# Decode attention plus MLP on one core: the attention's output weights loaded behind the last V tiles, and the MLP's last weight in three pieces

## The chip, the cores and the metric

The kernel runs on one core of one Trainium2 chip. The metric is the device time of the whole program in microseconds, taken over several executions; the profile is one further execution, and its span is about 2 us shorter than the timed figure. PE is the tensor engine, DVE the vector engine, ACT the scalar engine, and SP the sync engine, which issues the loads. The granted clock is the share of PE's full clock that its throttle let through. Times inside a profile are microseconds from the start of its span.

## The reference, cut to what matters

One decode step for 8 sequences: LayerNorm, attention with 32 query heads over 8 KV heads and the last 2048 cache positions, the output projection `wo`, then a block of LayerNorms and an MLP with weights `w3` and `w4`. Each sequence has one token, so the token-shift branch of the MLP block is zero and `w1`, `w2` drop out.

```python
def _A_ref(x, k_cache, v_cache, wq, wo):          # x: 8 x 1 x 512
    W = 2048                                      # last 2048 of 8192 positions
    q = (x @ wq) ...                              # 32 heads of 128
    k, v = k_cache[:, :, Sk-W:], v_cache[:, :, Sk-W:]
    p = softmax(q @ k.T * 128**-0.5)
    return (p @ v).reshape(8, 1, 4096) @ wo       # wo: 4096 x 512
def _B_ref(x, ...):
    x1 = x                                        # the shifted branch is zero
    return x1 + gelu(layernorm(x1) @ w3) @ w4     # w3: 512 x 1792, w4: 1792 x 512
h = x + _A_ref(layernorm(x), ...)
out = h + _B_ref(layernorm(h), ...)
```

K and V are 2 x 33.6 MB of the 79.2 MB that the kernel reads; wo is 4.2 MB, w3 and w4 1.8 MB each.

## The kernel before

All loads are issued from SyncE (SP) in one list. They go round through ten slots of 2 MiB; a load waits until the slot's former tile has been used. K and V come as 16 tiles each, four KV heads of one sequence per tile.

```python
WO_CUT = [0, 16, 24, 28, 32]      # heads of each wo piece
WO_HALF = H // 2
W4_CUT = [0, 8, 14]               # row groups (128 rows) of each w4 piece
V_CUT = [0, C // 2, C]            # the last V tile comes in two halves
order = [("k", 0), ("k", 1)]
for b in range(NB - 1):
    order += [("k", 2*b+2), ("v", 2*b), ("k", 2*b+3), ("v", 2*b+1)]
order += [("wo", 0), ("v", NTILE-2), ("v", NTILE-1), ("wo", 1), ("w3", 0), ("w4", 0)]

for n, (kind, t) in enumerate(order):             # on SP
    free_slot(n)                                  # waits for the user of order[n - 10]
    ...
    elif kind == "wo":                            # rows of 512 bf16, 1 KB each
        ... e.dma_start(dst[...], A_wo[h0*128:h1*128, :].rearrange("(h p) n -> p h n", p=128))
    elif kind == "w3":                            # rows of 3.5 KB
        e.dma_start(w3_sb, B_w3.rearrange("(k p) f -> p k f", k=KC)).then_inc(sem_w3, 16)
    else:                                         # rows of 2 KB
        for i in range(len(W4_CUT) - 1):
            c0, c1 = W4_CUT[i] // 2, W4_CUT[i+1] // 2
            e.dma_start(w4_dst[:, c0:c1, :], w4_rows[:, c0:c1, :]).then_inc(sem_w4[i], 16)
```

The end of the tensor engine's (PE) program, after the last softmax; the line numbers are those of the profile:

```python
# L530  P.V of V tile 14, then 15: 64 matmuls each of 16 columns
# L603  wo: 32 heads x 4 matmuls of 8 columns
for h in range(H):
    if h in WO_CUT:
        e.wait_ge(sem_wo[WO_CUT.index(h)], 16)
    for k in range(KC):
        e.matmul(hT_ps[:, k*B:(k+1)*B], wo_at(h)[:, k*128:(k+1)*128], oT_all[:, h, :], ...)
# L621  statistics of both LayerNorms; DVE and ACT make uT
# L663  w3: 14 x 4 matmuls of 8 columns
e.wait_ge(sem_w3, 16)
for fc in range(FC):
    for kc in range(KC):
        e.matmul(misc[:, H3...], w3_sb[:, kc, ...], uT[:, kc*B:(kc+1)*B], ...)
# ACT: gelu
# L684  the residual; L693  w4: 14 row groups x 2 matmuls of 256 columns
for fc in range(FC):
    if fc in W4_CUT:
        e.wait_ge(sem_w4[W4_CUT.index(fc)], 16)
    for j in range(NQ):
        e.matmul(fin_ps[32*j:32*j+B, :], gT[:, fc*B:(fc+1)*B], w4_sb[:, fc, j*DQ:(j+1)*DQ],
                 ..., tile_position=(0, 32*j))
# DVE and ACT copy the result out, SP stores it
```

## Time and profile before

| | before |
|---|---|
| timed, median (range) | 198.81 us (198.02 to 198.83), 3 runs |
| span of the profile | 196.6 us |
| bytes read | 79.18 MB, 403 GB/s over the span |
| busy: PE, DVE, ACT | 81%, 42%, 46% |

From the page of the kernel before, the span in 40 slices of 4.9 us: the granted tensor clock in tenths, the busy share of the 16 DMA engines in tenths, and what they moved.

```profile
PEclk9999999999996999999999699969999979755557
DMA  6999999999999999999999999999999999999990
GB/s 215 427 410 430 427 430 427 430 430 430 430 422 427 430 425 430 427 430 430 427 427 433 430 430 427 428 423 423 427 430 433 430 388 382 425 405 338 398 358 21
```

The DMA row shows 9 from the second slice to the last but one: the kernel is bound by its load queue for almost the whole span. The rate falls from 430 to between 338 and 425 GB/s near the end, where rows are 1 to 3.5 KB instead of 16 KB, though the engines stay busy. The Trainium skill (DMA: Bandwidth & Descriptors, "Why small descriptors are slow (HBM only)") gives a fixed overhead per packet as a cause; this trace agrees in direction (432 GB/s at 150 to 158 us with 16 KB rows, 352 at 179 to 184.5 with rows of 1 and 3.5 KB) but does not separate the causes. In slices 36 to 39 the clock row shows 5: half clock.

The end of the chain of waits of the kernel before (start, length, what):

```profile
174.82 9.25 DMA slots<-in_A_wo_dram
...
184.12 0.40 PE S_ps L603 x9
184.52 1.93 issue
186.46 0.34 PE S_ps L603 x7
...
191.76 2.64 PE b L693 x28
...
194.42 0.41 DVE xln_b L703
```

"issue" is time in which PE waited for nothing that the profile shows. The timeline of PE at the end of the kernel before (start, length, engine, line, operation, count, and in brackets the idle time ahead of it and what ended that):

```profile
174.16 1.88 PE L530 MATMUL misc<-pT_sb,slots 128*128 128x16 bf16 x64
176.23 1.02 PE L530 MATMUL misc<-pT_sb,slots 128*128 128x16 bf16 x32 [0.18 <-DMA slots<-in_A_v_cache_dram]
178.66 0.97 PE L530 MATMUL misc<-pT_sb,slots 128*128 128x16 bf16 x30 [1.41 <-DMA slots<-in_A_v_cache_dram]
179.86 0.23 PE L530 MATMUL misc<-pT_sb,slots 128*128 128x16 bf16 x2 [0.23 <-issue]
...
184.12 0.40 PE L603 MATMUL S_ps<-oT_all,slots 128*128 128x8 bf16 x9 [0.23 <-DMA slots<-in_A_wo_dram]
186.46 0.33 PE L603 MATMUL S_ps<-oT_all,slots 128*128 128x8 bf16 x7 [1.93 <-issue]
...
189.59 1.64 PE L663 MATMUL misc<-uT,slots 128*128 128x8 bf16 x56 [1.61 <-DVE uT L640]
...
191.58 2.79 PE L693 MATMUL b<-slots,gT 128*8 128x256 bf16 x28
```

V tile 15 is waited for twice (0.18 and 1.41 us), wo's last piece lands at 184.1, 1.93 us go to "issue" before wo's last seven matmuls, and the w4 matmuls (L693) run 2.79 us without a wait. SP's own timeline of the kernel before, around wo part 0:

```profile
125.03 0.39 SPq L266 DMA_DIRECT2D slots<-in_A_wo_dram  x1
127.27 36.10 SPq L260 DMA_DIRECT2D slots<-in_A_v_cache_dram  x1
```

The load of V tile 14 is issued at 127.27, but that instruction takes 36.10 us. The Trainium skill (Perfetto Trace Analysis, "DMA Instruction — HWDGE") says that the time recorded for such an instruction is the wait for the descriptor generator plus the generation, and not the data's movement. That fits here, though the profile does not show what is waited for: the load issued next after wo part 0 (2048 rows of 1 KB) is the one that takes so long, V tile 14.

### The profile page before, as it was taken

What the parts mean: (1) busy time and instruction counts of PE and PEld (TensorE: products, weight loads), DVE (VectorE), ACT (ScalarE), POOL (GpSimd) and SP (SyncE); (2) the same over time, 40 slices, a digit from 0 to 9 for tenths busy, and PEclk for the clock granted to TensorE, in tenths of its full rate; (3) what the DMA queues carried; (4) which work ended last, traced back from release to release, by engine and by line L of the source; (5) the groups of instructions that cost most, each with busy time, mean ns of one, the idle gap of its engine ahead of it and who ended that gap; (6) DMA issues with size and microseconds to landing.
All of it is one profiled execution on the core that took longest, in us unless ns stands there. A gap on an engine that the chain in (4) does not pass through costs nothing.

```text
span 196.6 us, 6327 instructions
## 1 busy us (share of the span) xinstructions
PE 159.2 (81%) x2808; PEld 118.4 (60%) x2808; DVE 82.4 (42%) x184; ACT 90.6 (46%) x109; POOL 4.7 (2%) x15
## 2 busy tenths in 40 slices
PE   2027999789999998988897889899979879395555
PEld 0027865566768675755675667677756656185553
DVE  7501445543463457335623473356336514330040
ACT  3300565945392648434753384457535635240040
POOL 8000000000000000000000000000000000000000
PEclk9999999999996999999999699969999979755557
DMA  6999999999999999999999999999999999999990
GB/s 215 427 410 430 427 430 427 430 430 430 430 422 427 430 425 430 427 430 430 427 427 433 430 430 427 428 423 423 427 430 433 430 388 382 425 405 338 398 358 21
DMA packets 10569, 79.57 MB, mean 405 GB/s; under 512 B 672, under 2 KB 4784, under 8 KB 6192
## 3 DMA queue, kind: packets, MB, share of 16 engines
q1 hardware_dynamic: 10544, 79.19, 96.5%
q8 instruction: 22, 0.36, 0.7%
q14 instruction: 3, 0.02, 0.0%
HBM read 79.18 MB, written 0.01 MB: 403 GB/s over the span
## 4 chain that ended last, share of the span: by engine, by line
DMA 56%; PE 28%; SPq 6%; issue 4%; DVE 3%; ACT 3%; ACTq 0%; DVEq 0%
DMA slots<-in_A_k_cache_dram 51%; PE kT_ps L406 16%; PE S_ps L438 6%; SPq L266 5%; DMA slots<-in_A_wo_dram 5%; PE misc L530 3%; ACT P_sb L472 1%; PE b L693 1%; ACT kT_sb L417 1%; PE misc L663 1%; DVE pT_sb L504 1%; PE S_ps L603 0%; PE S_ps L621 0%; DVE mtile L450 0%; SPq L258 0%
## 5 line engine op out<-in xcount | busy, mean ns | idle before, releaser
L417 ACT ACTIVATE kT_sb<-kT_ps 128x1024 bf16<-128x1024 bf16 x64 | 65.5, 1023 | 75.6 <-PE kT_ps L406 75.6
L406 PEld LDWEIGHTS kT_ps<-ident_b,slots 128*128 128x128 bf16 x1024 | 63.7, 104 | 30.0 <-issue 21.5
L406 PE MATMUL kT_ps<-ident_b,slots 128*128 128x128 bf16 x1024 | 73.2, 231 | 7.9 <-DMA slots<-in_A_k_cache_dram 7.9
L423 DVE COPY kT_sb<-kT_ps 128x1024 bf16<-128x1024 bf16 x64 | 43.4, 687 | 61.4 <-PE kT_ps L406 61.4
L438 PE MATMUL S_ps<-kT_sb,qstrip 128*32 128x512 bf16 x256 | 39.0, 614 | 0.0
L530 PEld LDWEIGHTS misc<-pT_sb,slots 128*128 128x128 bf16 x1024 | 27.3, 97 | 7.7 <-issue 5.9
L530 PE MATMUL misc<-pT_sb,slots 128*128 128x16 bf16 x1024 | 28.6, 170 | 3.7 <-DVE pT_sb L504 1.9
L472 ACT ACTIVATE P_sb<-S_ps,mtile 128x1024 bf16<-128x1024 f32 x16 | 17.8, 1113 | 4.8 <-DVE mtile L461 4.4
L406 PE MATMUL kT_ps<-ident_b,P_sb 128*128 128x128 bf16 x128 | 10.6, 231 | 6.6 <-ACT P_sb L472 5.5
L406 PEld LDWEIGHTS kT_ps<-ident_b,P_sb 128*128 128x128 bf16 x128 | 7.8, 103 | 12.0 <-issue 4.4
L504 DVE TENSOR_TENSOR pT_sb<-kT_ps,maskT 128x1024 bf16<-128x1024 bf16 x16 | 10.4, 684 | 0.1
L438 PEld LDWEIGHTS S_ps<-kT_sb,qstrip 128*32 128x32 bf16 x256 | 6.0, 94 | 6.5 <-issue 1.2
L537 DVE TENSOR_TENSOR oT_all<-misc,rL 128x32 bf16<-128x32 f32 x8 | 2.4, 300 | 16.0 <-PE misc L530 16.0
L585 ACT ACTIVATE std<-var,eps_t 128x8 f32<-128x8 f32 x1 | 0.3, 301 | 14.3 <-DVE var L636 14.3
L450 DVE TENSOR_REDUCE mtile<-S_ps 128x1 f32<-128x512 f32 x8 | 5.5, 692 | 3.1 <-PE S_ps L438 3.1
L361 PE MATMUL S_ps<-xlnT,slots 128*128 128x8 bf16 x128 | 3.6, 168 | 3.6 <-DMA slots<-in_A_wq_dram 3.6
L361 PEld LDWEIGHTS S_ps<-xlnT,slots 128*128 128x128 bf16 x128 | 3.5, 104 | 3.6 <-issue 3.6
L603 PE MATMUL S_ps<-oT_all,slots 128*128 128x8 bf16 x128 | 3.9, 168 | 2.2 <-issue 1.9
L341 PE MATMUL b<-ident_b,xln_b 8*128 8x8 bf16 x4 | 0.3, 175 | 6.4 <-DVE xln_b L318 6.4
L603 PEld LDWEIGHTS S_ps<-oT_all,slots 128*128 128x128 bf16 x128 | 3.6, 104 | 2.3 <-issue 2.0
L481 DVE TENSOR_TENSOR lsum<-lcol 128x1 f32<-128x1 f32 x8 | 1.3, 158 | 8.0 <-ACT P_sb L472 8.0
L341 PEld LDWEIGHTS b<-ident_b,xln_b 8*128 8x128 bf16 x4 | 0.2, 116 | 7.3 <-DVE xln_b L318 7.3
(75 smaller groups left out, 59.8 us busy)
## 6 DMA issues: line engine op xcount, KB each, us to landing
slots<-in_A_k_cache_dram SPq DMA_DIRECT2D x16, 2048.0 KB, 41.5
slots<-in_A_v_cache_dram SPq DMA_DIRECT2D x15, 2048.0 KB, 43.3
slots<-in_A_wq_dram SPq DMA_DIRECT2D x1, 4096.0 KB, 12.2
slots<-in_A_wo_dram SPq DMA_DIRECT2D x1, 2048.0 KB, 43.8
slots<-in_A_v_cache_dram SPq DMA_DIRECT2D x2, 1024.0 KB, 13.6
slots<-in_B_w_dram SPq DMA_DIRECT2D x1, 1792.0 KB, 11.6
slots<-in_A_wo_dram SPq DMA_DIRECT2D x1, 1024.0 KB, 16.5
slots<-in_A_wo_dram SPq DMA_DIRECT2D x2, 512.0 KB, 13.0
```

The source lines that it names most:

```text
L266: e.dma_start(dst[:, f0:f0 + (h1 - h0) * D].rearrange("p (h n) -> p h n", n=D), A_wo[h0 * 128:h1 * 128, :].rearrange("(h p) n -> p h n", p ...
L361: ins = e.matmul(S_ps[:, 0, h * B:(h + 1) * B], wq_v[:, kc, h * DH:(h + 1) * DH], xlnT[:, kc * B:(kc + 1) * B], start=(kc == 0), stop=(kc ...
L406: ins = e.matmul(kT_ps[n % 2][:, c * 128:(c + 1) * 128], src[:, c * 128:(c + 1) * 128], ident_b[:, :], is_transpose=True)
L417: e.activation(kT_sb[:, i % NKT, 0:W // 2], kT_ps[step_of[("k", i)] % 2][:, 0:W // 2], ACT.Copy).then_inc(sem_Elo, 1)
L423: e.tensor_copy(kT_sb[:, i % NKT, W // 2:W], kT_ps[step_of[("k", i)] % 2][:, W // 2:W]).then_inc(sem_Ehi, 1)
L438: ins = e.matmul(S_ps[32 * gl:32 * (gl + 1), b % 2, :], qstrip[:, b, GL * gq + gl, o:o + 32], kv[:, gl, :, :], start=(gq == 0 and qi == 0) ...
L450: ins = e.tensor_reduce(mtile[:, 2, 0:1], S_ps[:, j, :], AX.X, ALU.max)
L472: e.activation(P_sb[:, half * W // 2:(half + 1) * W // 2].rearrange("r (k g) -> r k g", g=GL), s_rep, ACT.Exp, bias=mtile[:, j, 0:1], scal ...
L504: e.tensor_tensor(pT_sb[:, half * hc:(half + 1) * hc, :], kT_ps[n % 2][:, half * W // 2:(half + 1) * W // 2].rearrange("p (c x) -> p c x", ...
L530: ins = e.matmul(ot, slots[:, slot, c * DH:(c + 1) * DH], pt[:, cc, :, o:o + R], start=(n == 0), stop=(n == C - 1), skip_group_check=True)
L537: e.tensor_tensor(oT_all[:, :, b].rearrange("p (q g r) -> p g q r", g=GL, r=R), misc[:, OT].rearrange("p (g q r) -> p g q r", g=GL, r=R), ...
L603: ins = e.matmul(hT_ps[:, k * B:(k + 1) * B], wo_at(h)[:, k * 128:(k + 1) * 128], oT_all[:, h, :], start=False, stop=(h == H - 1), skip_gr ...
```

## The change: intent and diff

wo part 0 (2 MiB) is not needed until attention is over, but it was loaded ahead of the last two V tiles. The change puts it behind them, so that the last P·V no longer waits. And w4 gets a small last piece, so that less work remains when the last bytes land.

```diff
-        sem_w4 = [S(f"sem_w4_{i}") for i in range(2)]
+        sem_w4 = [S(f"sem_w4_{i}") for i in range(3)]
...
-        W4_CUT = [0, 8, 14]
+        W4_CUT = [0, 8, 12, 14]
...
-        order += [("wo", 0), ("v", NTILE - 2), ("v", NTILE - 1), ("wo", 1), ("w3", 0), ("w4", 0)]
+        order += [("v", NTILE - 2), ("v", NTILE - 1), ("wo", 0), ("wo", 1), ("w3", 0), ("w4", 0)]
```

The instructions of PE, DVE and ACT keep their order; only SP's list changes, and PE gets one more wait, before w4's row group 12.

## The prediction

> **What bounds the kernel now.** The load queue, then a latency chain. By slices, the 16 DMA engines are about 99% busy until just before the end; 79.2 MB at 405 GB/s is 195 us of a 196.6 us span. The last weight bytes (w4) move until about 192.6 us (packet records), so this change, which keeps every byte, has 192.6 us as its floor, plus a short tail.
>
> The end of the chain of waits (us from start): the last K tile lands 158.9; last scores 168.9; max, exp, transposes until 174.1 (compute, no DMA); P·V of tile 14 174.2 to 176.0; tile 15 waits for its two halves (176.2, 178.7) and its last two matmuls for "issue" (179.86); wo matmuls 180.7 to 183.9, the last wo piece arrives 184.1, then a gap of 1.9 us put down to "issue", done 186.8; LayerNorm until 189.5; w3 matmuls to 191.2 (w3 had landed about 188.4); w4 matmuls 191.58 to 194.37, at half clock and without a wait; eviction and output store.
>
> **The "issue" gaps.** PE's instructions come in blocks. The Trainium skill (Runtime: NRT & Kernel Launch, Instruction fetch mechanics) says 16 KiB blocks of 256 instructions, prefetched one ahead. The trace agrees: 22 packets of 16 KiB on the instruction queue, and counting 256 PE records back from the gap at 186.46 gives block starts 179.86 and 173.88. The fetches moved at 177.44 and 184.23, each 3.6 to 4.4 us after the block before began, and the block was usable 2.2 to 2.4 us later. So a block takes about 6 us under this DMA load; three of these blocks are wanted faster.
>
> **What the change does.** PE, DVE and ACT programs stay the same. wo part 0 (2 MB, 1 KB rows, about 5 us) moves from before V14 to after V15. So V14 and V15 land about 5 us earlier (estimate 169 and 173.5), before softmax is ready at 174. That removes waits of about 0.2 + 1.4 us in P·V. wo part 0 then lands about 178.4, wo's last piece, w3 and w4 no earlier than before. The small last w4 piece costs one more issue (about 0.5 us on SP, hidden) and shortens what remains after the last bytes from 12 matmuls (1.2 us) to 4 (0.4 us).
>
> **On the critical path.** P·V could end at 178.1 instead of 180.1, but its last two matmuls need the block requested at 173.9, usable 177.6 to 179.9. The wo matmuls still cannot finish before 184.1 + 0.7. If the later block comes in time, that 1.9 us gap goes, and the chain then hits w3's landing (188.4) and w4's first piece (about 191.2): worth only 0.4 us at half clock, about 1.2 us with a full clock. If the fetch stays as slow, the gain is 0 to 0.5 us. SP's long issue (36 us behind wo's descriptors in before) moves to after V15, without starving the engines.
>
> **Predicted:** 198.0 us, 0.4% less; range 197.0 to 199.0. Faster by over 2%: 0.02; within 2%: 0.96; slower: 0.02.
>
> **Would show it right:** V15 no longer waited for; last w4 byte at 192 to 193 us; wo's last pieces about 184; mean GB/s of the span unchanged. An issue gap in P·V's last two matmuls or in wo, smaller or moved. The 36 us issue at V14 gone, a long one at wo.
>
> **Would make it wrong:** a load queue that runs empty while wo's small descriptors are generated (DMA share under 0.9 after 165 us: slower by 1 to 3 us); the K15 landing moving (skew of the engines); PE's clock becoming full from about 177 us, so that the w4 matmuls end right after the last piece (faster by about 1 us); longer instruction fetches behind 1 KB packets (slower by up to 1 us).

## The result and the profile after

| | before | after |
|---|---|---|
| timed, median (range), 4 runs each | 198.74 us (198.02 to 198.83) | 198.54 us (198.39 to 198.72) |
| ratio, 95% interval | | 0.9996 (0.9978 to 1.0014) |
| span of the profile | 196.6 us | 196.5 us |

A ratio is the mean time of one kernel's fast runs over that of the other's in the same rounds, so it is not quite the ratio of the medians quoted. The change is worth nothing that can be measured. The clock and DMA rows of the page, after:

```profile
PEclk9999999976999999996999699999996999955556
DMA  6999999999999999999999999999999999999980
```

The chain of waits after:

```profile
176.20 2.57 issue
...
178.91 12.10 DMA slots<-in_B_w_dram
...
191.14 3.17 PE b L693 x28
...
194.33 0.41 DVE xln_b L703
```

The end of the chain has another form. It no longer passes through wo; it comes out of a load of w4 (issued 178.91, landed 191.01) and goes straight into the w4 matmuls. The step ahead of it, from the "issue" gap in P·V to that load, is not a dependency: the wait that SP passes there is for P·V of tile 11, the former tile of the slot, and SP had been issuing without a pause (w3 from 177.27 to 178.86). In run e3, without that gap, the load is issued at the same 178.92. PE's timeline after:

```profile
172.67 3.53 PE L530 MATMUL misc<-pT_sb,slots 128*128 128x16 bf16 x126
178.77 0.22 PE L530 MATMUL misc<-pT_sb,slots 128*128 128x16 bf16 x2 [2.57 <-issue]
...
184.18 0.40 PE L603 MATMUL S_ps<-oT_all,slots 128*128 128x8 bf16 x9 [0.77 <-DMA slots<-in_A_wo_dram]
185.64 0.33 PE L603 MATMUL S_ps<-oT_all,slots 128*128 128x8 bf16 x7 [1.07 <-issue]
...
188.77 1.64 PE L663 MATMUL misc<-uT,slots 128*128 128x8 bf16 x56 [1.61 <-DVE uT L640]
...
191.14 3.15 PE L693 MATMUL b<-slots,gT 128*8 128x256 bf16 x28 [0.21 <-DMA slots<-in_B_w_dram]
```

Read against the same lines of before: the first 126 matmuls of P·V run without a wait, and the V waits (1.6 us) are gone. But the last two wait 2.57 us for "issue" where before they waited 0.23. The last wo piece is waited for until 184.18, as before. The second "issue" gap is 1.07 us instead of 1.93. wo's last matmuls begin 0.8 us earlier, the w4 matmuls 0.44 us earlier, and these now wait 0.21 us for w4's first piece. They then need 3.15 us instead of 2.79, and everything ends 0.1 us earlier than before.

P·V began 1.5 us earlier than before in this profile (172.67 against 174.16). This pair does not show that the change did it: in the kernel before, a stretch at half clock (159.72 to 163.14) fell on the matmuls of the last K tile, and in the changed kernel none did; and in other profiles with the new order P·V began anywhere from 172.7 to 174.4. The old order can hold it up, though: in run e2 it waited 0.75 us for V tile 14.

SP's timeline after:

```profile
126.73 6.95 SPq L258 DMA_DIRECT2D slots<-in_A_v_cache_dram  x2
133.72 43.51 SPq L266 DMA_DIRECT2D slots<-in_A_wo_dram  x4
```

The long issue moved from the V tile to wo, 43.51 us for the four pieces together, where it delays nothing that the profile shows: wo's last piece lands at 184.13, before at 184.07. The engines were not starved: the DMA row of the page after shows 9 (90% or more) in every slice of that time.

### The profile page after: what moved, and what is told of

It reads as the page before. It is cut to its first block, busy times and chain, and to the rows that moved or that the text cites. A ratio compares the mean times of both kernels' runs of the same rounds, so it can differ in the third digit from the quotient of the medians.

```text
span 196.5 us, 6328 instructions
## 1 busy us (share of the span) xinstructions
PE 159.4 (81%) x2808; PEld 118.9 (61%) x2808; DVE 82.4 (42%) x184; ACT 90.6 (46%) x109; POOL 4.7 (2%) x15
## 4 chain that ended last, share of the span: by engine, by line
DMA 57%; PE 31%; issue 4%; ACT 3%; DVE 3%; SPq 0%; ACTq 0%; DVEq 0%
DMA slots<-in_A_k_cache_dram 51%; PE kT_ps L406 17%; PE S_ps L438 7%; DMA slots<-in_B_w_dram 6%; PE misc L530 5%; ACT P_sb L472 2%; PE b L693 2%; ACT kT_sb L417 1%; DVE mtile L450 1%; DVE pT_sb L504 1%; DVE mtile L461 0%; DVE mrow L452 0%; DVE mrow L454 0%; DVE xln_b L703 0%; DVE mrow L457 0%
## 5 line engine op out<-in xcount | busy, mean ns | idle before, releaser
L406 PEld LDWEIGHTS kT_ps<-ident_b,slots 128*128 128x128 bf16 x1024 | 64.5, 105 | 28.1 <-issue 21.4
L406 PE MATMUL kT_ps<-ident_b,slots 128*128 128x128 bf16 x1024 | 74.1, 233 | 6.2 <-DMA slots<-in_A_k_cache_dram 6.1
L423 DVE COPY kT_sb<-kT_ps 128x1024 bf16<-128x1024 bf16 x64 | 43.5, 687 | 59.9 <-PE kT_ps L406 59.9
L438 PE MATMUL S_ps<-kT_sb,qstrip 128*32 128x512 bf16 x256 | 38.3, 613 | 0.0
L294 DVE TENSOR_SCALAR ident_f<-iota_f 128x128 f32<-128x128 f32 x1 | 3.9, 3924 | 1.5 <-POOL iota_f L200 1.5
```

What stands on the lines that cost most here:

```text
L294: e.tensor_single_scalar(ident_f[:], iota_f[:], 0.0, ALU.is_equal)
L406: ins = e.matmul(kT_ps[n % 2][:, c * 128:(c + 1) * 128], src[:, c * 128:(c + 1) * 128], ident_b[:, :], is_transpose=True)
L423: e.tensor_copy(kT_sb[:, i % NKT, W // 2:W], kT_ps[step_of[("k", i)] % 2][:, W // 2:W]).then_inc(sem_Ehi, 1)
L438: ins = e.matmul(S_ps[32 * gl:32 * (gl + 1), b % 2, :], qstrip[:, b, GL * gq + gl, o:o + 32], kv[:, gl, :, :], start=(gq == 0 and qi == 0) ...
```

## The experiments

Three accounts were set against each other.

- **A.** The w4 matmuls end the kernel: 14 row groups at half clock, 0.21 us each, from the landing of w4's *first* piece (or from gelu). Later w4 bytes come in time.
- **B.** The last w4 bytes end the kernel (the prediction's floor).
- **C.** PE's instruction blocks come late and eat the gain.

Each run was timed in five rounds against the kernel before.

### Run e1_order_only and run e12_order_again: only the new order

```diff
-        W4_CUT = [0, 8, 12, 14]
+        W4_CUT = [0, 8, 14]          # against the changed kernel; sem_w4 accordingly
```

> Only the new load order, w4 in its two old pieces (8 and 6 rows of 128). Theory A (the w4 matmuls at half clock, 14 x 0.21 us after the first w4 piece lands, end the kernel, and no later byte is waited for): same as the changed kernel, 0.998 to 1.001 of before; the w4 matmuls show no wait at their ninth row. Theory B (the last w4 bytes end the kernel): 0.3 to 0.8 us slower than the changed kernel, because 6 rows are left after the last bytes. Tile 15 of V is not waited for in either; an issue gap of 2 to 3 us stands in the P.V of tile 15 in either.

Measured: median 199.40 us, 1.0021 of before (0.9996 to 1.0046). The times fell in two groups, two at 198.4 and four at 199.3 to 199.8; the profile is of the quick group. In it, V is not waited for, the two issue gaps are 2.57 and 2.10 us, and the w4 matmuls have no wait at their ninth row. The time alone would fit B, so the same kernel was run again.

> The order-only kernel once more, unchanged, because its times fell in two groups (198.4 and 199.3 to 199.8) and only a run of the quick group was profiled. If the order alone is really slower with w4 in two pieces (theory B), the ratio is again 1.002 or more and the profile has a wait for DMA before the ninth w4 row. If theory A holds, a profile of the slow group shows the w4 matmuls without such a wait, all at half clock (2.95 us or more), or starting later behind a longer issue gap; a ratio of 0.999 to 1.001 would make the first result a matter of the chip or the moment.

Measured: 1.0001 (0.9971 to 1.0032), median 199.40, again in two groups (198.1 to 198.5 and 199.4 to 199.5). This time a slow execution was profiled (span 197.7 us). PE's timeline of that one:

```profile
180.29 0.22 PE L530 MATMUL misc<-pT_sb,slots 128*128 128x16 bf16 x2 [2.43 <-issue]
...
187.16 0.33 PE L603 MATMUL S_ps<-oT_all,slots 128*128 128x8 bf16 x7 [2.61 <-issue]
...
192.28 3.16 PE L693 MATMUL b<-slots,gT 128*8 128x256 bf16 x28
```

Two issue gaps, 2.43 and 2.61 us, then the w4 matmuls, which start 1.1 us later than in the changed kernel. They run 3.16 us, all at half clock and with no wait, although w4's last byte had moved at 192.6 here as in before (192.6) and after (192.7). So in a slow execution account C holds: from the last K tile on, the late instruction blocks are on the chain, and no load is. But the clock is the other half. Against the quick profile of e1, the same kernel, the w4 matmuls start 0.63 us later (192.28 against 191.65) and take 0.56 us longer (3.16 against 2.60), because there the clock became full at 193.53 and here not before the end. In these runs the order alone gained nothing. The kernel before has some such executions too (up to 199.8 us in the same rounds), but fewer: 4 of its 22 times in the rounds of e1 and e12 are above 199.2 us, and 8 of these 12. Why was not settled.

### Run e2_cut_only: only w4 in three pieces

```diff
-        W4_CUT = [0, 8, 14]
+        W4_CUT = [0, 8, 12, 14]      # against the kernel before; sem_w4 accordingly
```

> Only w4 in three pieces, the old load order. Theory A: 0.999 to 1.001 of before, w4 matmuls without a wait and 2.8 to 3.0 us long at half clock. Theory B: 0.3 to 0.8 us faster than before. Issue gaps as in before: small at the end of P.V, about 1.9 us in the wo matmuls.

Measured: 0.9995 (0.9977 to 1.0013). Its w4 matmuls:

```profile
191.31 3.15 PE L693 MATMUL b<-slots,gT 128*8 128x256 bf16 x28 [0.46 <-DMA slots<-in_B_w_dram]
```

They start at 191.31 behind the first piece, and the row groups then stand 0.21 us apart to the end, with no wait for either later piece. The issue gap in wo was 0.35 us there, not 1.9: it differs from run to run. The small last piece is worth nothing that can be measured here.

### Run e3_shift64: the instruction blocks moved

```diff
+            for _ in range(64):
+                e.matmul(S_ps[:, 1, 0:8], zrow_b[0:1, :], x_sb[0:1, 0:8], start=True, stop=True)
             e.wait_ge(sem_wq, 16)
```

> The changed kernel with 64 small matmuls (zeros) added where PE waits for wq, about 10 to 13 us from the start. They move every later 256-instruction boundary 64 matmuls earlier in the program, so the blocks that come late are asked for before softmax and after V14. Both late gaps put down to issue (2.6 us in P.V, 1.1 us in wo) should shrink to under 0.5 us. Theory C (instruction fetch is where the gain went): 1 to 2 us faster than the changed kernel. Theories A and B: wo's last piece still lands at 184.2, w3 at about 188.6 and the first w4 piece at about 191.1, so the w4 matmuls start at the same 191.1 and the gain is 0 to 0.2 us.

Measured: 198.27 us, 0.9971 (0.9953 to 0.9989). PE's timeline of this run:

```profile
173.57 3.59 PE L532 MATMUL misc<-pT_sb,slots 128*128 128x16 bf16 x128
...
180.64 0.32 PE L605 MATMUL S_ps<-oT_all,slots 128*128 128x8 bf16 x6 [0.16 <-issue]
...
188.58 1.66 PE L665 MATMUL misc<-uT,slots 128*128 128x8 bf16 x56 [2.53 <-DMA slots<-in_B_w_dram]
...
191.23 2.72 PE L695 MATMUL b<-slots,gT 128*8 128x256 bf16 x28 [0.47 <-DMA slots<-in_B_w_dram]
```

P·V now runs its 128 matmuls in one stretch, and the issue gap in wo is 0.16 us. wo is done early enough that the w3 matmuls wait for w3 (188.58), and the w4 matmuls still wait for w4's first piece (191.23). Their start is not earlier than in the changed kernel (191.14), as A and B said; they end earlier because the clock became full at 193.37, shortly before their end. So C explains the gaps, but taking them out gives only what the next landing allows: 0.27 us less than the changed kernel by the medians, with intervals that overlap, not the 1 to 2 us of C. None of the five times is in a slow group (198.15 to 198.48); the four of the changed kernel were not either.

The blocks can be followed in the trace. The packets of 16 KiB on the instruction queue are the fetches. Counting 256 PE records (weight loads, matmuls, waits) from one gap to the next gives the block starts, to within a record or two, because weight loads overlap matmuls.

```
run                     block before starts  fetch moves   block starts   gap
before                  173.88               177.44        179.86         0.23
before                  179.86               184.23        186.46         1.93
changed                 172.28               176.38        178.77         2.57
changed                 178.77               183.22        185.64         1.07
order only, slow        173.93               177.90        180.29         2.43
order only, slow        180.29               184.79        187.16         2.61
changed + 64 matmuls    175.28               178.38        180.65         0.16
```

In every row a block starts 2.2 to 2.4 us after its fetch began to move, and the fetch moves 3.1 to 4.5 us after the block before it started. So in these late blocks PE gets 256 instructions in no less than 5.4 to 6.9 us. The Trainium skill (Runtime: NRT & Kernel Launch, "Instruction fetch mechanics") describes blocks of 256 instructions fetched while the one before runs; these rows agree with that. Its remark that the cost is mostly hidden holds for 20 of the 22 block crossings in the kernel before, which leave no gap, and not for the last two (0.23 and 1.93 us). P·V and wo want their blocks faster: 128 matmuls of P·V took 3.59 us in run e3.

### Run e4_w4_short: 0.75 MiB of w4 left out

```diff
-        W4_CUT = [0, 8, 12, 14]
+        W4_CUT = [0, 8]
...
-                                   w4_sb[:, fc, ...
+                                   w4_sb[:, fc % 8, ...
```

> The changed kernel with only the first 8 of w4's 14 row groups loaded (0.75 MiB less, about 1.8 us of the load queue); the other 6 use the first rows again, so the result is wrong on purpose. Theory A: no more than 0.3 us faster than the changed kernel. Theory B: 1.0 to 1.8 us faster.

Measured: 198.51 us, 0.9992 (0.9968 to 1.0015), the changed kernel's 0.9996. (The comparison with the reference passed all the same.) The last w4 byte moved at 190.7 instead of 192.7, and this is the line of the w4 matmuls:

```profile
191.10 3.15 PE L693 MATMUL b<-slots,gT 128*8 128x256 bf16 x28
```

The same 3.15 us from the same 191.1. B is out: with 0.75 MiB fewer bytes at the very end, the kernel ends at the same time.

### Run e5_before_shift64: the old order without the late blocks

```diff
# against the kernel before: the same 64 matmuls ahead of the wait for wq
```

> The kernel before with the 64 added early matmuls, so old load order and old w4 pieces without the late instruction blocks. If the load order had a value of its own that the fetch gaps hid, this should be 0.5 to 1 us slower than the changed kernel with the same 64 matmuls (0.997 of before). If the order's gain is swallowed by what lands later whatever the order (wo's last piece 184.2, w3 188.5, first w4 piece 191.1), it should be the same as that one within 0.2 us: about 0.997 to 0.999 of before, w4 matmuls from about 191.2.

Measured: 198.53 us, 0.9993 (0.9978 to 1.0008). The intervals of this run and of e3 overlap, so the times leave open whether the new order is worth 0.2% once the gaps are gone; 0.5 us was the least expected if it had a value of its own, and the measured ratios differ by 0.0022, about 0.4 us. The profile says where the difference lies:

```profile
188.51 1.66 PE L665 MATMUL misc<-uT,slots 128*128 128x8 bf16 x56 [2.80 <-DMA slots<-in_B_w_dram]
...
191.07 3.23 PE L695 MATMUL b<-slots,gT 128*8 128x256 bf16 x28 [0.39 <-DMA slots<-in_B_w_dram]
```

In the old order too, the w3 matmuls wait for w3 (188.51) and the w4 matmuls for the first piece (191.07, against 191.23 in e3). What the order saves upstream is lost at these two landings. This profile ends 0.35 us later than that of e3, in part by a 0.1 us wait at w4's ninth row, the rest because all its rows ran at half clock.

### Run e6_first_piece: a small first piece of w4

```diff
-        W4_CUT = [0, 8, 12, 14]
+        W4_CUT = [0, 4, 8, 12, 14]   # plus the 64 matmuls
```

> The changed kernel with the 64 added early matmuls and w4 in four pieces of 4, 4, 4 and 2 rows, so that the first piece is small. Theory A (the end is the landing of the first piece plus 14 x 0.21 us at half clock): the w4 matmuls begin when gelu is done, about 190.7 instead of 191.2, and end 0.3 to 0.5 us earlier: 0.994 to 0.997 of before. Theory B (last bytes): no gain over the run with the 64 matmuls alone (0.997).

Measured: 197.87 us, 0.9961 (0.9947 to 0.9974). The w4 matmuls start at 190.78 with gelu, 0.4 us earlier, as A said. They then wait 0.2 us at the third piece. The gain over e3 is 0.1% and the intervals overlap. The profile does not decide between A and B: the clock became full at 192.91 here, and the last two rows start at 193.26, right behind the landing of the last piece (193.22).

### Run e7_clock: the tensor engine kept busy

```diff
+        h3_wide = kT_ps[0][:, 0:1024].bitcast(dt.float32)
+        idle_ps = kT_ps[1][:, 0:1024].bitcast(dt.float32)
+        def keep_busy(e, n):
+            for _ in range(n):
+                e.matmul(idle_ps, ident_b[:, :], kT_sb[:, 0, 0:512], start=True, stop=True)
...              # one ahead of the wait for the LayerNorm input, five after the statistics
-                    ins = e.matmul(misc[:, H3.start + fc * B:H3.start + (fc + 1) * B],
+                    ins = e.matmul(h3_wide[:, fc * 32:(fc + 1) * 32].rearrange("p (r b) -> p r b", r=4),
...
-                                   uT[:, kc * B:(kc + 1) * B],
+                                   bass.AP(..., offset=kc * B, ap=[[KB, 128], [0, 4], [1, B]]),
                 # plus all of e6; gelu reads columns 0 to 7 of each 32
```

> As the run with the small first piece, and the tensor engine is kept busy: the w3 matmuls have 32 columns instead of 8 (repeats that nobody reads), and six idle 512-column matmuls stand where it waits for the LayerNorm and w3. If the half clock of the last 24 us comes from small, sparse matmuls, the clock is full before the w4 matmuls, which then take 0.11 us a row and wait for their last pieces: end at about 193 us, 0.7 to 1.2 us before the run with the small first piece: 0.989 to 0.993 of before. If the clock stays at half, no gain or up to 0.3 us lost to the added work.

Measured: 197.57 us, 0.9944 (0.9930 to 0.9957), the lowest of all, though the intervals of e6, e10 and e11 overlap it. The 0.7 to 1.2 us under e6 did not come: it is 0.3 us by the medians, and five of the six times lie under all six of e6. Busy time by stretch (stretch, its length, PE, PEld, DVE, ACT, POOL, granted clock, DMA share, GB/s), first the changed kernel, then this run:

```profile
184.50:189.00 4.50, 1.32 (x21) 1.01 (x19) 1.67 (x11) 1.12 (x3) 0.00 (x0) 0.50 1.04 410
...
191.00:194.40 3.40, 3.15 (x28) 1.77 (x28) 0.07 (x1) 0.07 (x1) 0.00 (x0) 0.50 0.15 57
```

```profile
184.50:189.00 4.50, 4.03 (x31) 1.80 (x32) 2.24 (x13) 1.98 (x4) 0.00 (x0) 0.50 1.03 408
189.00:190.70 1.70, 1.70 (x64) 1.51 (x60) 0.00 (x0) 0.25 (x1) 0.00 (x0) 0.86 1.04 402
190.70:193.80 3.10, 2.21 (x30) 0.92 (x28) 0.08 (x1) 0.10 (x2) 0.00 (x0) 1.00 0.34 129
```

The first row of each is the same stretch: PE is busy 4.03 instead of 1.32 us. The clock then becomes full at about 189.5 and stays so to the end of the matmuls. In e6 the half-clock stretch began at the same point (172.43, here 172.41) and lasted until 192.91. A w4 row now takes 0.11 us, and the matmuls wait for their pieces:

```profile
190.76 1.26 PE L705 MATMUL b<-slots,gT 128*8 128x256 bf16 x16
192.71 0.97 PE L705 MATMUL b<-slots,gT 128*8 128x256 bf16 x12 [0.68 <-DMA slots<-in_B_w_dram]
```

Now the last bytes end the kernel: the last piece lands at 193.25, and two rows follow. In e6's profile they did so too, since the clock became full just in time, and the w4 matmuls of both end together (193.65 and 193.67). The Trainium skill (TensorE: Matmul & The Clock Gate, Part 1) says that the clock is half by default, that about 3.4 us of sustained activity release it, and that the windows of 3413 ns run freely. On the windows the trace agrees: the half-clock stretch of the changed kernel, from 171.02 to 194.91, is 23.89 us, seven times 3.413. No run here tests the default. The traces also show that a stage need not look idle to count so. Here is one window of the kernel before, with wo's matmuls of 8 columns, and then the last window at half clock of this run, with 512 and 32 columns:

```profile
180.20:183.62 3.42, 3.05 (x112) 3.07 (x113) 0.22 (x1) 0.00 (x0) 0.00 (x0) 0.50 0.97 326
```

```profile
186.07:189.48 3.41, 3.00 (x31) 1.28 (x31) 1.86 (x11) 1.98 (x4) 0.00 (x0) 0.50 1.04 408
```

PE was busy about 3.0 us in each; after the first the clock stayed at half, after the second it became full. So busy time alone does not decide it: in e1, PE was busy for the whole window from 173.05 to 176.47, mostly with P·V's 16-column matmuls, and the clock stayed at half too. Whether the wide w3 matmuls or the idle ones did it was not separated.

### Runs e10_clock_two and e11_clock_three: the small last piece at full clock

```diff
-            W4_CUT = [0, 8, 14]          # e10, else as e7
+            W4_CUT = [0, 8, 12, 14]      # e11
```

> New load order, 64 early matmuls, the tensor engine kept busy as in the clock run, and w4 in its two old pieces (8 and 6 rows). At full clock a w4 row takes 0.11 us, so now the last bytes should end the kernel: the second piece lands at about 193.2 and 6 rows (0.65 us) follow, end of the w4 matmuls about 193.9 to 194.0.

> The same with w4 in the changed kernel's three pieces (8, 4 and 2 rows), the only difference from the run with two pieces. If the half clock is what made the small last piece worthless in the change, it is worth 0.3 to 0.5 us here: the last 2 rows follow the landing at about 193.2 and the w4 matmuls end at about 193.5 to 193.7, with a wait for DMA before the last two rows in the trace. If it is worthless at full clock too, the two runs end within 0.1 us of each other.

Measured: e10 197.95 us, 0.9959 (0.9944 to 0.9974); e11 197.65 us, 0.9952 (0.9932 to 0.9971). The intervals overlap, so the profiles are compared; first e10, then e11:

```profile
192.97 0.82 PE L705 MATMUL b<-slots,gT 128*8 128x256 bf16 x12 [0.78 <-DMA slots<-in_B_w_dram]
```

```profile
192.54 0.60 PE b L705 x8
...
193.18 0.40 PE b L705 x4
```

With two pieces, six rows follow the last landing (192.92), and the matmuls end at 193.8. With three, only two rows follow it (193.14), and they end at 193.6. So in this pair the small last piece is worth 0.2 us at full clock, at the lower edge of what was expected or under it (the medians differ by 0.30 us): the last of three pieces landed 0.2 us later than the last of two. At half clock it was worth nothing that could be measured.

### Runs e8_w3_split and e9_both: w3 in two pieces

```diff
+        W3_CUT = [0, 8, 14]
...
+                if fc in W3_CUT:
+                    e.wait_ge(sem_w3[W3_CUT.index(fc)], 16)
                 # e8: plus e6; e9: plus e7 with three idle matmuls after the statistics
```

> As the run with the small first piece, and w3 comes in two pieces (8 and 6 of 14 column groups), each waited for by itself. With the fetch gaps gone, the LayerNorm is done at about 187.3 and waits for all of w3 until 188.5; now the first w3 matmuls start at about 187.3 and all end at about 189.4 instead of 190.2. The w4 matmuls then start at about 190 and, at half clock, end about 193.0: 0.3 to 0.7 us less than the run with the small first piece, 0.990 to 0.994 of before. Rows of 2048 and 1536 bytes instead of 3584 may cost 0.1 us on the queue.

> All of it: new order, 64 early matmuls, w4 in four pieces, w3 in two, tensor engine kept busy. If the last w4 bytes are now the floor (192.9 to 193.3, as in the clock run), splitting w3 adds nothing: within 0.2 us of the clock run, 0.993 to 0.996 of before. If something earlier still held the clock run back, another 0.3 us or more.

Measured: e8 198.24 us, 0.9980 (0.9965 to 0.9994); e9 198.18 us, 0.9960 (0.9944 to 0.9976). Both miss. The w3 matmuls do start at 187.4, and the w4 matmuls at 190.0. But then they wait for the second and third piece of w4; the third piece in e8:

```profile
190.06 1.02 PE L700 MATMUL b<-slots,gT 128*8 128x256 bf16 x8
191.25 1.02 PE L700 MATMUL b<-slots,gT 128*8 128x256 bf16 x8 [0.17 <-DMA slots<-in_B_w_dram]
192.49 1.44 PE L700 MATMUL b<-slots,gT 128*8 128x256 bf16 x12 [0.22 <-DMA slots<-in_B_w_dram]
```

From 192.49 six rows are left, at half clock 1.3 us. The earlier start cannot be used: past this point the pieces set the pace. And in e8 the clock stayed at half to the end, where in e6 it became full at 192.91. In e9 it became full only at 192.1, and its times are spread (197.5 to 198.4). e7 has the lowest time; at 0.9944 it beats both kernels by about half a per cent.

## Why the prediction was right or wrong, point by point

- **The time.** Predicted 198.0, range 197.0 to 199.0, within 2%: 198.54 measured. Right in class and range; the expected gain of 0.4% did not come (0.04%, interval -0.14% to +0.22%). The range also holds the kernel before (198.74), so that lying in it says little about the mechanism.
- **V's wait goes.** Right: 1.6 us of waits for V tile 15 are gone.
- **P·V's last two matmuls need their instruction block.** Right in kind, and shown by e3. The block's time was estimated at up to 6.0 us from its request; it took 6.5 us (172.28 to 178.77), so the gap was 2.57 us. P·V as a whole, from its first matmul to its last, took 6.3 us instead of 5.9, although 1.6 us of waits were gone from it; it ended 1.1 us earlier only because it began 1.5 us earlier in this profile.
- **wo's last piece, w3 and w4 do not land earlier.** Right: wo's last piece 184.13 against 184.07, and last w4 byte 192.7 against 192.6.
- **"the chain then hits w3's landing (188.4) and w4's first piece (about 191.2)".** Right where the gaps are gone: in e3 and e5 the w3 matmuls wait for w3 (188.6 and 188.5) and the w4 matmuls for the first piece (191.2 and 191.1). The changed kernel waits for the second alone (191.14).
- **"has 192.6 us as its floor", with the small piece shortening "what remains after the last bytes from 12 matmuls (1.2 us) to 4 (0.4 us)".** This step was wrong. In the changed kernel nothing is left to shorten: at half clock the 14 rows take 3.15 us from 191.14, longer than the rest of w4 needs to land (192.99). Removing 0.75 MiB of it (e4) changed nothing. The last bytes end the kernel where the clock is full before them (e7, e10, e11, and e6 by its profile); there the small piece is worth about 0.2 us. With the cuts of the two kernels, the most that they cost at half clock in any profile is the 0.1 us wait at the ninth row in e5.
- **The size: "worth only 0.4 us at half clock".** The w4 matmuls did start 0.44 us earlier, with the later gap not gone but 0.9 us shorter. What the sum left out is that the clock can change inside this stage: in the profile of before it became full at 193.86, three rows before their end, and after it did not (194.91), so that they took 3.15 us instead of 2.79. That took 0.36 of the 0.44 us. It is a matter of where the clock's free windows fall, and differs between executions, as the start does: in e2, with the old order, the w4 matmuls began at 191.31. The near agreement of this one pair of profiles is chance; the timed runs only say that the gain is under about 0.2%.
- **No starving of the load queue.** Right: the DMA row shows 9 in every slice while SP is stuck 43.5 us in wo's issues.

What stays open: why a fetch moves 3.1 to 4.5 us after its request under this load. The table gives the times, but no run changed the load queue's packets to show their part. Also open are the order's worth without gaps to better than 0.2%, and why the order-only kernel fell in the slow group more often than the others.

## What to carry to other kernels

Before moving a load to remove a wait, follow the chain on to the next landings behind it: a wait removed upstream is worth only what the latest of those allows, and PE's own instruction blocks are one of them. A smaller last piece pays only if the work after the *first* piece is faster than the rest of the bytes; check the granted clock in that stage before counting on its matmuls. A few wide matmuls in the waits ahead of a short tail brought the full clock 3.4 us forward here and about 0.3 us of time (e7 against e6), where the order of the loads alone gained nothing that could be measured.

## What the Trainium skill lacked or had wrong

- Runtime: NRT & Kernel Launch, "Instruction fetch mechanics", calls the crossing of a 16 KiB block "mostly hidden", and says PE holds 128 KiB (2048 instructions), while the same section speaks of two lines. Here 22 blocks were fetched one at a time, for 5774 PE records. 20 crossings left no gap; but a late block under a full load queue started 5.4 to 6.9 us after the one before, and where PE wanted it faster, gaps of up to 2.6 us were not hidden.
- TensorE: Matmul & The Clock Gate, Part 1, gives a time of sustained activity, but not what share of it, or how wide the matmuls, releases the clock. Here 8-column matmuls that kept PE busy 3.05 us of one window left it at half; with 32-column and 512-column matmuls, busy 3.00 us of one, it became full. With three idle matmuls instead of five after the statistics (e9, 185.32 to 188.74) 3.05 us were not enough.
- No page gives how many descriptors a load queue takes before the issuing instruction blocks. Here a V tile's issue took 36.10 us behind a load of 2048 rows of 1 KB; the median of the K and V issues was 0.54 us.
